# First norm's means on TensorE from a transposed X, and one new issue order up to the first convolution

## The chip, the cores and the metric

The kernel runs on one core of one Trainium2 chip. The time is the device time of that core in microseconds (us) for one launch: of the kernel before, three runs took 423.18, 423.9 and 425.21 us, with a median of 423.9.

## What is computed

Two pairs of layers on a sequence x of S = 2048 tokens with D = 512 channels (one batch). Each layer adds to x its function of the layer norm of x, with no learned scale:

```python
x = x + A(layernorm(x)); x = x + B(layernorm(x))      # twice, same weights

def A(u):      # state space layer: a long convolution per channel
    dt = exp(log_dt)[:, None]
    K = einsum("dn,dnl,dn->dl", C, exp((dt * A)[:, :, None] * l), dt * B).real   # D x 2048, 128 complex states
    return irfft(rfft(pad(u)) * rfft(pad(K)))[:2048] + u * Dskip

def B(x):      # attention: 32 heads of 16, 8 keys at distances 0, 2, .. 14 behind each token
    q, k, v = x @ wqkv
    return softmax(q . k[gathered] / 4, masked) . v[gathered] @ wo

def layernorm(x):
    m = mean(x); return (x - m) / sqrt(var(x) + 1e-5)
```

## The kernel before

**Layout.** x lies in four tiles X (128 x 4 x 512): token 16 p + j is row j of partition p, so that "row j" (j from 0 to 15) is a 128 x 512 slab. The normed rows go into tiles N of the same shape. The convolution of layer A is a two-stage Fourier transform: the first stage (L636) multiplies each row j by a table F1 on TensorE (PE); its result is copied into a large tile Z; then, by groups of channels, come transposes (L248), the second stage (L263), the product with the kernel's spectrum Kt (L275), and the way back (L291, L295 and the y rows at L336 to L344). The B layer begins with the copies at L1549.

**Generating the convolution kernel.** All that comes before the first convolution is in `kgen`. A ladder of squarings makes the powers of exp(dt A) up to 2048 (words m, q, l, b). From these, for each quarter c of 128 channels, tables U and V are built by doubling: DVE multiplies (L502, L504; for the last V steps, whose names end in n, L483), and the real and imaginary sums are either added on DVE (L514, words that begin with %), or summed by PE with an identity matrix (L528, words with +) and copied back by ACT (L535, L538, words with =). U and V have two buffers, so quarters 2 and 3 write where quarters 0 and 1 were read. The products lie in Z's space until the tables are done; so no z copy may come before the last table word.

Then PE multiplies V by U (words p{c}{q}, L568 and L572, four per quarter); ACT copies two products at a time out to KT (k{c}{m}, L579). The second k of a quarter also issues four transfers of KT to DRAM, two on SP and two on POOL (L587), and POOL, behind them, one transfer back into the tile `rows` (L590). The spectra s{c}{i} (L601, L606) multiply rows by tables G0 and G1 on PE; o and e copy and combine them (ACT L617, L622 to L625, DVE L630) and store them on SP (L611). Spectra 1 to 6 take ten matmuls (L601) and one ACT copy; the others five (L606), an ACT copy and two DVE sums.

**The first norm.** Statistics of row j are word n{j}: on DVE by bn_stats (L179 to L181), or, with an a behind it, on ACT in two passes, one that sums the row into its mean (L184), one that sums the squares of the differences (L185). r0 and r1 make the inverse deviation of eight rows each (ACT, L190 and L191), a0 and a1 the bias (DVE, L196); N{j} applies both to a row (ACT L202 or DVE L204). f{j} is the first stage on PE, z{j} its copy to Z (DVE L641, ACT L643 for halves, ACT L645 whole).

**The order of the work.** It is written by hand in the string KGEN (L353 to L370). `run` (L769) takes its words one by one within a manual schedule and issues the instructions of each; so the order of the string is the order on each engine, and an instruction that waits holds all behind it on the same engine. Words that begin with @ are the steps of the first convolution: @T0 is the first transpose. Words w and W are matmuls on the identity that write a PSUM tile ahead of its use (L550 to L556).

**Loads.** After the parameters, SP's queue issues X (L144), F1 (L1663) and G1 (L419); G0 follows at the word prep (L447). The weights and constants of later layers come on SP and POOL.

Of the kernel before, what the change touches and what calls it, by code (L numbers as in the profile page):

```python
# [14 lines left out]
F32 = mybir.dt.float32  # L15
# [160 lines left out]
def first_norm_row(nc, small, st, Xg, j, on_act):  # L176
    x, mv = Xg[j // 4][:, j % 4, :], st["mv"][:, j, :]
    if not on_act:
        nc.vector.bn_stats(st["stats"][:, j, :], x)  # L179
# [4 lines left out]
    nc.scalar.activation(junk[:], x, ACT.Identity, scale=1.0 / D, accum_out=mv[:, 0:1])  # L184
    nc.scalar.activation(junk[:], x, ACT.Square, scale=-1.0, bias=mv[:, 0:1], accum_out=st["m2"][:, j:j + 1])  # L185
# [130 lines left out]
def a_layer(nc, tc, C, Xg, Ng, kt_dram, layer, Z, es_z, a=None):  # L316
# [10 lines left out]
    def y_rows(g, hf, row, ps, add):  # L327
# [25 lines left out]
KGEN = ("m0 q0 b0 x1 l0 m1 q1 x0 t l1 b1 x3 x2 q2 m2 b2 l2 x5 m3 U4p:1 q3 U4:0 l3 b3 %U4:0 u:1 m4 q4 u:0 l4 b4 m5 q5 U2p:0 l5 +U2p:0 b5 "  # L353
# [30 lines left out]
def kgen(nc, tc, C, prm, kt_dram, Zf, norm_row, norm_rstd, norm_apply, norm_apply_row, norm_tiles, load_rest, es_a, es_y, open_conv):  # L384
    everything = KGEN.split()
    with ExitStack() as es:
# [32 lines left out]
        nc.sync.dma_start(Gt[1][:], C["G_h"].ap()[1])  # L419
# [89 lines left out]

        def sum_dve(name, c):  # L510
            prod, out, hn, f, size = sums[name, c]
            for r in range(2):
                x, y = (prod[i][:, (r + i) % 2].rearrange("n (h f c) -> n h f c", h=hn, f=f) for i in range(2))
                nc.vector.tensor_tensor(out(r), x, y, ALU.add if r else ALU.subtract)  # L514
# [35 lines left out]
        def warm(tile, cols):  # L550

            flat = tile[:].rearrange("n a b -> n (a b)")
            while cols > 0:
                n = min(cols, 512)
                nc.tensor.matmul(flat[:, 0:n], C["ident"][:], C["ident"][:].unsqueeze(1).to_broadcast([128, n // 128, 128]), start=True, stop=True)
                cols -= n  # L556
# [18 lines left out]
        def product_out(c, m):  # L575
# [3 lines left out]
            nc.scalar.copy(KT[:, :, :, m * 16:(m + 1) * 16, :].rearrange("v w t h f -> v (w t) h f"),  # L579
# [5 lines left out]
            for t in range(2):  # L585
                for b in range(2):
# [4 lines left out]
                                                   C["rows_dram"].ap()[c].rearrange("t b w v x -> (w v) (t b) x"))  # L591

# [40 lines left out]
        def first_stage(j):  # L633
            ps = tiles["f", j] = psum()[0].tile([128, 2, D], F32, name="ps_s1", tag="psk")
            for r in range(2):
                nc.tensor.matmul(ps[:, r, :], C["F1"][:, j, r, :], C["Ng"][j // 4][:, j % 4, :], start=True, stop=True)  # L636

        def first_stage_out(j, part):
            src = tiles["f", j][:].rearrange("k r (c e g) -> k r c g e", c=16, e=GE)
            if part == "v":  # L640
                nc.vector.tensor_copy(C["z_view"][:, 1, j], src[:, 1])  # L641
            elif part == "a":
                nc.scalar.copy(C["z_view"][:, 0, j], src[:, 0])  # L643
            else:
                nc.scalar.copy(C["z_view"][:, :, j], src)  # L645

# [40 lines left out]
        for c in range(4):  # L687
# [48 lines left out]
        for j in range(16):  # L736
            for a in ("", "a"):
                word(f"N{j}{a}", lambda j=j, a=a: norm_apply_row(j, bool(a)), f"a{j // 8}", "prep")
            word(f"n{j}", lambda j=j: norm_row(j, False))
            word(f"n{j}a", lambda j=j: norm_row(j, True))  # L740
        tables = [w for c in range(4) for w in in_quarter(c, *steps)]
        for j in range(16):
            word(f"f{j}", lambda j=j: first_stage(j), f"N{j}a" if f"N{j}a" in everything else f"N{j}")
            for part in ("", "a", "v"):
                word(f"z{j}{part}", lambda j=j, part=part: first_stage_out(j, part), f"f{j}", *tables)
        for full in everything:
            if full[0] in "wW":
                word(full, lambda full=full: warm((product_tile if full[0] == "w" else spectrum_tile)(int(full[1]), int(full[2])), int(full.split(":")[1])), "x5")
# [866 lines left out]
def kernel(  # L1615
# [40 lines left out]
    n1 = {}  # L1656

    def load_rest():
# [4 lines left out]
        nc.sync.dma_start(C["F1"][:], C["F1_h"].ap())  # L1663
# [65 lines left out]
```

## Time and profile before

| what | us |
|---|---|
| median of three runs | 423.9 |
| the profiled execution | 424.25 |
| its span, first to last instruction | 422.4 |
| first ACT statistics row (L184) begins | 45.92 |
| first spectrum (L601) begins | 69.55 |
| first transpose of the convolution (L248) begins | 119.53 |
| first copy of the B layer (L1549) begins | 153.69 |

The mean granted clock of TensorE in that execution was 0.992 of full speed. Engines are named PE (TensorE matmul), PEld (its weight load), DVE (VectorE), ACT (ScalarE), POOL (GpSimd) and SP (SyncE, which issues transfers); a q behind a name is its instruction queue. A row of the timeline has the start, the duration, the engine, the line, the operation, the tiles written and read with shapes, and a count; in square brackets the idle time before it and what ended that. A row of groups has the total busy time, the mean of one in ns, and the idle time before. In the windows view each row is a stretch of time with the busy time of each engine in it.

### The profile page before, as it was taken

The numbers are of one execution on the slowest core, as the hardware profiler recorded it, in microseconds if no ns is written. First come the engines' busy times: TensorE is split into PE (matmuls) and PEld (weight loads), VectorE is DVE, ScalarE is ACT, GpSimd is POOL, SyncE is SP. The second block draws the span as 40 slices with busy tenths as digits, with TensorE's granted clock in tenths as the row PEclk, the third lists the DMA queues.
The fourth block names the chain that finished last, engine by engine and source line by source line (L and its number), as shares of the span: only waits on it lengthen the run. The fifth ranks groups of instructions, "written<-read, shape, count | busy, mean of one in ns | idle before, by whom it ended". The sixth has DMA issues, their size and how long they took to land.

```text
span 422.4 us, 12235 instructions
## 1 busy us (share of the span) xinstructions
PE 379.3 (90%) x5120; PEld 259.1 (61%) x5120; DVE 398.4 (94%) x730; ACT 332.7 (79%) x600; POOL 26.0 (6%) x68
## 2 busy tenths in 40 slices
PE   1157898999989999999999999889999999997996
PEld 1023585676458755587866575278855686875663
DVE  5999999999889979899999999999989999999994
ACT  6999998998979989766665699989988676663542
POOL 5000011001210000002020000000000001200000
PEclk9999999999999999999999999999999999998999
DMA  8900001254889960005480028239300009350022
GB/s 241 424 29 0 2 12 42 76 166 104 250 245 276 259 213 2 2 2 98 81 174 3 2 64 238 102 107 288 107 0 4 2 2 166 73 115 2 2 102 101
DMA packets 25822, 44.09 MB, mean 104 GB/s; under 512 B 7317, under 2 KB 17238, under 8 KB 25126
## 3 DMA queue, kind: packets, MB, share of 16 engines
q1 hardware_dynamic: 22918, 38.09, 31.9%
q0 software_dynamic: 1888, 4.56, 5.0%
q8 instruction: 40, 0.66, 0.6%
q10 hardware_dynamic: 960, 0.66, 0.5%
q14 instruction: 16, 0.13, 0.1%
HBM read 29.04 MB, written 6.95 MB: 85 GB/s over the span
## 4 chain that ended last, share of the span: by engine, by line
PE 46%; DVE 25%; ACT 7%; DMA 6%; issue 4%; SPq 2%; DVEq 0%; ACTq 0%
PE ps_qk L1207 10%; DVE prodpv L1403 9%; PE ps_v L1294 5%; DVE prodqk L1257 4%; PE vp L291 3%; PE psg L601 3%; PE Lp L1279 3%; PE po L1413 3%; PE ps_o L1443 2%; DVE Z L504 2%; DVE pab L275 2%; DMA Kt<-kt_scratch 2%; PE psk L568 2%; DMA V<-V 2%; ACT Z L1496 2%
## 5 line engine op out<-in xcount | busy, mean ns | idle before, releaser
L1403 DVE TENSOR_TENSOR prodpv<-V,Lsb 128x2048 bf16<-128x2048 bf16 x64 | 75.3, 1221 | 0.7 <-DMA V<-V 0.4
L1207 PE MATMUL ps_qk<-xnT,wqk 128*128 128x512 bf16 x256 | 59.9, 379 | 0.0
L1255 DVE TENSOR_TENSOR prodqk<-qT,N 128x1024 bf16<-128x1024 bf16 (+3 forms) x88 | 42.6, 544 | 1.9 <-ACT N L1210 1.9
L1257 DVE TENSOR_TENSOR prodqk<-qT,N 128x1024 bf16<-128x1024 bf16 (+3 forms) x56 | 40.4, 765 | 0.3 <-ACT qT L1210 0.2
L1413 PEld LDWEIGHTS <-prodpv 128*128 128x128 bf16 x1024 | 35.3, 100 | 7.2 <-DVE prodpv L1403 2.0
L275 DVE TENSOR_TENSOR pab<-xc,Kt 128x2048 bf16<-128x2048 bf16 (+1 forms) x34 | 38.8, 1154 | 0.7 <-issue 0.4
L1413 PE MATMUL po<-halves,prodpv 128*128 128x64 bf16 x1024 | 38.1, 196 | 0.9 <-DVE prodpv L1403 0.9
L1207 PEld LDWEIGHTS <-wqk 128*128 128x128 bf16 x256 | 23.7, 98 | 23.5
L269 ACT CAST xc<-xp 128x1024 bf16<-128x1024 f32 (+1 forms) x34 | 34.6, 1033 | 2.2 <-PE xp L263 1.9
L291 PEld LDWEIGHTS <-pab 128*128 128x128 bf16 x512 | 30.4, 98 | 7.0 <-DVE pab L275 3.5
L291 PE MATMUL vp<-sb_IC,pab 128*128 128x128 bf16 x512 | 33.6, 219 | 0.6 <-DVE pab L275 0.3
L1279 PEld LDWEIGHTS <-prodqk 128*128 128x128 bf16 x1024 | 29.8, 96 | 5.5 <-DVE prodqk L1257 2.5
L295 ACT CAST VT<-vp 128x1024 bf16<-128x1024 f32 (+1 forms) x31 | 32.7, 1065 | 0.6 <-PE vp L291 0.6
L1443 PE MATMUL ps_o<-wo_t,oT 128*128 128x512 bf16 x128 | 33.0, 379 | 0.0
L1279 PE MATMUL Lp<-sb_bones,prodqk 128*128 128x8 bf16 x1024 | 30.5, 166 | 1.0 <-DVE prodqk L1257 0.8
L528 PE MATMUL psadd<-Z,sb_ident 128*128 128x384 bf16 (+3 forms) x75 | 18.7, 337 | 13.1 <-DVE Z L504 7.9
L1294 PE MATMUL ps_v<-wv,xnT 128*128 128x256 bf16 x256 | 30.4, 272 | 0.0
L1424 ACT CAST oT<-po 128x512 bf16<-128x512 f32 x32 | 17.7, 589 | 13.8 <-PE po L1413 13.7
L1210 ACT CAST N<-ps_qk 128x512 bf16<-128x512 f32 x32 | 18.7, 587 | 12.1 <-PE ps_qk L1207 11.9
L1160 DVE BATCH_NORM_STATS2 ln_stats<-X 128x6 f32<-128x512 bf16 x39 | 24.9, 682 | 2.7 <-ACT X L1549 2.7
L1301 ACT CAST V<-ps_v 128x512 bf16<-128x512 f32 x32 | 18.2, 588 | 10.9 <-PE ps_v L1294 10.8
L1294 PEld LDWEIGHTS <-xnT 128*128 128x128 bf16 x256 | 24.2, 98 | 3.2
(202 smaller groups left out, 837.8 us busy)
## 6 DMA issues: line engine op xcount, KB each, us to landing
Kt<-kt_scratch SPq DMA_DIRECT2D x60, 256.0 KB, 5.5
kt_scratch<-ks SPq DMA_DIRECT2D x32, 128.0 KB, 3.0
G<-c_G SPq DMA_DIRECT2D x2, 1536.0 KB
V<-V SPq DMA_DIRECT2D x8, 288.0 KB, 7.8
X<-in_A_u_dram SPq DMA_DIRECT2D x4, 512.0 KB, 4.8
F1Tsb<-c_F1T SPq DMA_DIRECT2D x2, 1024.0 KB
V<-V SPq DMA_DIRECT2D x4, 512.0 KB
V<-V POOLq DMA_DIRECT2D x4, 384.0 KB, 8.3
```

Source lines behind the costliest of these rows:

```text
L269: nc.scalar.copy(xcs[cg][:, gs].rearrange("q g o l -> q (g o l)"), xps[cg][:].rearrange("q h n -> q (h n)")[:, gs.start * 128:gs.stop * 128])
L275: nc.vector.tensor_tensor(pabs[cg][:, gs], xcs[cg][:, gs].to_broadcast([128, gs.stop - gs.start, 2, 128]), kts[cg][:, gs], ALU.mult)
L291: a.last_pe = nc.tensor.matmul(vp[:, g, :], pabs[cg][:, gs.start + g, ab, :], C["IC"][:, ab, :], start=(ab == 0), stop=(ab == 1))
L295: copy(dst[..., parts(cg)[part]], vps.pop((cg, part))[:].rearrange("k g (q e) -> k q e g", e=GE))
L1207: nc.tensor.matmul(t.ps[:], wqk[:, ct, f0:f0 + 128], x_group(g)[:, :, ct], start=(ct == 0), stop=(ct == 3))
L1255: nc.vector.tensor_tensor(b.pr[:, u:u + 2 * n, 1 - halves_of[0], :], q, cols(kT[i][:, starts[0]:starts[0] + n * 128]), ALU.mult)
L1257: nc.vector.tensor_tensor(b.pr[:, u:u + 2 * n].rearrange("f u a q -> f a u q")[:, ::-1], q.unsqueeze(1).to_broadcast([128, 2, 2 * n, 64]), ...
L1279: nc.tensor.matmul(t.Lp[:, w, u % 2, u // 2, :], b.pr[:, u].rearrange("f a q -> f (a q)"), bones[:], start=False, stop=(t.parts == W // 2 ...
L1294: nc.tensor.matmul(t.ps[:, jj, :], tokens(ct, jp * 2 + jj, c), wv[:, ct, fp * 256:(fp + 1) * 256], start=(jj + ct == 0), stop=(jj == 1 and ...
L1403: nc.vector.tensor_tensor(t.p2[:, c:c + k, 0:nj, :].rearrange("p c j (d h) -> p c j d h", d=DH), m.V2[i // 2][:, c0 + c:c0 + c + k, r0:r0 ...
L1413: nc.tensor.matmul(po[jj // k][:, jj % k, c, :], t.p2[:, c - c0, jj, :], fold, start=(first and c == c0 and jj % k == 0), stop=(last and c ...
L1443: nc.tensor.matmul(t["ps"][:], m.oT[:, ft, j * 128:(j + 1) * 128], wo_t[:, ft, :], start=(start and ft == lo), stop=(ft == 3 or kept and f ...
```

## The change

1. The ACT pass that made the mean of a row (L184) is gone. Instead, sixteen transposing transfers on SP, issued behind the loads of X, write each row j transposed (512 channels by 128 tokens, in four blocks) into space that G1 (rows 0 to 11) and F1 (rows 12 to 15) take later. A new word xm sums them: 64 matmuls, each with a 128 x 128 block as weights and one column of ones, four of them added up per row, into one PSUM tile of 16 columns. A new word xo copies that to the means with a scale of 1/512 on ACT, and then issues the loads of G1 and F1 on SP. The norm rows, the spectra and the first stage wait for xo. All 16 norm rows are on ACT now (15 and one on DVE before).
2. The identity matmuls that fill PE are given as `~columns` and are issued with the next fresh PSUM tile: 8,704 columns, where there were 14,720.
3. Thirteen N rows are on ACT and three on DVE (8 and 8 before); of the z copies by halves, ten are on ACT and six on DVE (8 and 8), with each half to be placed by itself. One table copy (u:1) goes from DVE to ACT, one (B:0) from ACT to DVE. k may be given to DVE by a letter, which the new order doesn't do.
4. The string KGEN is new from its first word to the end of the first convolution.

The places of the order of which the prediction speaks, before:

```
... v16xn:0 p02 n14a +0U512p:1 +1U512p:1 v16x:1 n0a n2 =1U512p:1 l10 prep p00 n4a
k01 v16yn:1 =0U512p:1 p01 %v16x:1 v2:2 n1a U4p:2 Aa:2 %v2:2 p12 k00 c0 +U4p:2 ua:2 =U4p:2 v4p:2 Ba:2 U2:2 %U2:2 p13 +v4p:2 n6a
U256:2 k11 p10 =v4p:2 U1p:2 p11 w23:256 %U256:2 v2p:3 n7a +v2p:3 r0 =v2p:3 +U1p:2 Aa:3 v8p:2 =U1p:2 U1024:2 k10 U4:3 s01 ua:3
%U1024:2 +1v8p:2 o01 v4:3 %U4:3 a0 ...
... v16xn:2 N3a +U1024p:3 %U1:3 =U1024p:3 N5a p22 v8:3 o10 k21 U512:3 p21 n13a %v8:3 N1a %U512:3 p20 n11a k20 v16x:3 s11 n10a %v16x:3
s13 o11 o13 p31 r1 v16y:3 N6a a1 p30 N0a %v16y:3 k30 s00 N12 N13 f6 N8 N11 z6 p32 o00 e13 p33 N15a f1 k31 ... z2v s31 o30 @T0
```

and after:

```
... %U512:0 xm xo n2a v16yn:0 prep +1v8p:1 +0v8p:1 U512p:1 n5a =1v8p:1 n3a =0v8p:1 n9a v16x:1 v16xn:0 p02 p03 p00
+0U512p:1 n14a k01 n0a +1U512p:1 =0U512p:1 =1U512p:1 p01 v2:2 U4p:2 %v2:2 v16yn:1 n4a p13 +U4p:2 ua:2 n1a Aa:2 =U4p:2 v4p:2 U2:2
%v16x:1 %U2:2 n6a k00 n7a s01 o01 r0 c0 n8a p12 +v4p:2 p10 =v4p:2 Ba:2 n12a k11 s03 o03 U256:2 a0 ...
... a1 %v8:3 N14a %U512:3 v16yn:2 N12a v16x:3 v16y:3 %v16x:3 %v16y:3 v16xn:2 p22 p20 p21 p23 k20 N6a s11 k21
N13a o11 N8a N3a N15a s13 p33 p32 p31 p30 k31 f12 s00 o13 k30 ... f0 z0 z141a @T0
```

The diff, cut to its core:

```diff
     junk = small.tile([128, D], BF, name="n1_junk", tag="junk", bufs=1)
-    nc.scalar.activation(junk[:], x, ACT.Identity, scale=1.0 / D, accum_out=mv[:, 0:1])
     nc.scalar.activation(junk[:], x, ACT.Square, scale=-1.0, bias=mv[:, 0:1], accum_out=st["m2"][:, j:j + 1])
...
         load_rest()
-        nc.sync.dma_start(Gt[1][:], C["G_h"].ap()[1])
+        flat = [Gt[1][:].rearrange("n a b -> n (a b)"), C["F1"][:].rearrange("n a b c -> n (a b c)")]
+        xT = [flat[j // 12][:, j % 12 * D:(j % 12 + 1) * D].rearrange("n (t p) -> n t p", t=4) for j in range(NJ)]
+        for j in range(NJ):
+            nc.sync.dma_start_transpose(xT[j], C["x_row"](j))
...
+        def fresh(tile):
+            warm(tile, late.pop("fill", 0))
+            return tile
...
+        def row_sums():
+
+            ps = tiles["m"] = fresh(psum()[1].tile([128, 2, 512], F32, name="psm", tag="psg"))
+            for j in range(NJ):
+                for t in range(4):
+                    nc.tensor.matmul(ps[:, 0, j:j + 1], xT[j][:, t, :], C["signs"][:, 0:1], start=(j + t == 0), stop=(j == NJ - 1 and t == 3))
+
+        def row_sums_out():
+            nc.scalar.activation(C["mean"](), tiles["m"][:, 0, 0:NJ], ACT.Copy, scale=1.0 / D)
+            nc.sync.dma_start(Gt[1][:], C["G_h"].ap()[1])
+            nc.sync.dma_start(C["F1"][:], C["F1_h"].ap())
+        word("xm", row_sums, "x5")
+        word("xo", row_sums_out, "xm")
...
-            word(f"n{j}", lambda j=j: norm_row(j, False))
-            word(f"n{j}a", lambda j=j: norm_row(j, True))
+            word(f"n{j}", lambda j=j: norm_row(j, False), "xo")
+            word(f"n{j}a", lambda j=j: norm_row(j, True), "xo")
...
-        nc.sync.dma_start(C["F1"][:], C["F1_h"].ap())
```

More of the change, by code (lines that the diff above doesn't have):

```diff
@@ L508, in step, with warm @@
                 C["powers_used"] = last
+        def warm(tile, cols):
+            flat = tile[:].rearrange("n a b -> n (a b)")
+            while cols > 0:
+                n = min(cols, 512)
+                nc.tensor.matmul(flat[:, 0:n], C["ident"][:], C["ident"][:].unsqueeze(1).to_broadcast([128, n // 128, 128]), start=True, stop=True)
+                cols -= n
+        def fresh(tile):
+            warm(tile, late.pop("fill", 0))
+            return tile
         def sum_dve(name, c):
@@ L546, in spectrum_tile @@
             if ("s", c, i) not in tiles:
-                tiles["s", c, i] = psum()[1].tile([128, 2, 512], F32, name="psg", tag="psg")
+                tiles["s", c, i] = fresh(psum()[1].tile([128, 2, 512], F32, name="psg", tag="psg"))
             return tiles["s", c, i]
[L550 to L556, printed above, removed]
         def product(c, q):
@@ L573, in product, with product_out @@
                                          skip[:, s0 + hl - 7:s0 + hl + 1, :], start=False, stop=False)
-        def product_out(c, m):
+        def product_out(c, m, copy):
             if ("KT", c) not in tiles:
@@ L633, in first_stage @@
         def first_stage(j):
-            ps = tiles["f", j] = psum()[0].tile([128, 2, D], F32, name="ps_s1", tag="psk")
+            ps = tiles["f", j] = fresh(psum()[0].tile([128, 2, D], F32, name="ps_s1", tag="psk"))
             for r in range(2):
@@ L639, in first_stage_out @@
             src = tiles["f", j][:].rearrange("k r (c e g) -> k r c g e", c=16, e=GE)
[L640 to L644, printed above, removed]
+            if not part:
                 nc.scalar.copy(C["z_view"][:, :, j], src)
+                return
+            r = int(part[0])
+            (nc.scalar.copy if part[1] == "a" else nc.vector.tensor_copy)(C["z_view"][:, r, j], src[:, r])
         word("y", lambda: nc.scalar.copy(Ln[:], lads[7][:, 1, :]), "l6")
@@ L725, in kgen @@
             for m in range(2):
-                word(f"k{c}{m}", lambda c=c, m=m: product_out(c, m), f"p{c}{2 * m}", f"p{c}{2 * m + 1}", "prep")
+                for v, copy in (("", nc.scalar.copy), ("v", nc.vector.tensor_copy)):
+                    word(f"k{c}{m}{v}", lambda c=c, m=m, copy=copy: product_out(c, m, copy), f"p{c}{2 * m}", f"p{c}{2 * m + 1}", "prep")
             for i in range(4):
-                word(f"s{c}{i}", lambda c=c, i=i: spectrum(c, i), f"k{c}0", f"k{c}1")
+                word(f"s{c}{i}", lambda c=c, i=i: spectrum(c, i), *[w for w in everything if w.rstrip("v") in (f"k{c}0", f"k{c}1")], "xo")
                 word(f"o{c}{i}", lambda c=c, i=i: spectrum_odd(c, i), f"s{c}{i}")
@@ L1656 @@
     n1 = {}
+    C["x_row"] = lambda j: Xg[j // 4][:, j % 4, :]
+    C["mean"] = lambda: n1["st"]["mv"][:, :, 0]
     def load_rest():
```

16 lines of the change are left out of this document (8 added, 8 removed), and 33 rows, old and new, of the table KGEN.

## The prediction

> **What bounds the kernel now.** First the busy totals of the page, for the whole span; then the windows view, because a total is a mean over stages; then single rows of the timeline where the change puts a wait.
>
> ```profile
> PE 379.3 (90%) x5120; PEld 259.1 (61%) x5120; DVE 398.4 (94%) x730; ACT 332.7 (79%) x600; POOL 26.0 (6%) x68
> ```
>
> ```profile
> core 0: us, PE busy (x) PEld busy (x) DVE busy (x) ACT busy (x) POOL busy (x), PEclk, DMA share, GB/s
> 50.00:60.00 10.00, 10.00 (x289) 9.00 (x289) 9.93 (x17) 9.77 (x23) 0.00 (x0) 1.00 0.01 3
> 90.00:100.00 10.00, 10.00 (x183) 7.22 (x180) 9.97 (x18) 9.04 (x22) 1.87 (x3) 1.00 0.64 189
> 110.00:120.00 10.00, 9.39 (x48) 4.39 (x46) 8.39 (x14) 8.58 (x15) 0.57 (x3) 1.00 0.89 264
> ```
>
> The change touches only what lies ahead of the first convolution's end. There, from 50 to 100 us, DVE is never free (9.93 and 9.97 of 10 us), ACT nearly so, and PE is full. A stage in which three engines are all full has no slack for a wait that stops all three; removing work from one of them gives only what the other two can follow. Five rows mark the stage: the last DVE table product, the first spectrum behind it, the first transpose of the convolution (@T0), its first ACT copy, and the first ACT copy of the B layer.
>
> ```profile
> 97.65 1.23 DVE L514 TENSOR_TENSOR Vtab<-Z 128x960 bf16<-128x960 bf16 x2
> 98.22 1.27 PE L606 MATMUL psg<-G,rows 128*128 128x512 bf16 x5
> 119.53 1.07 PE L248 MATMUL pt<-sb_ident,Z 128*128 128x128 bf16 x16 [0.23 <-DVE Z L641]
> 121.69 1.01 ACT L269 CAST xc<-xp 128x1024 bf16<-128x1024 f32 x1 [1.22 <-PE xp L263]
> 153.69 1.01 ACT L1549 CAST X<-ps_y 128x1024 bf16<-128x1024 f32 x1 [0.72 <-PE ps_y L344]
> ```
>
> So the tables end at 97.65 + 1.23 = 98.9 us, @T0 follows 20.6 us later, and the B layer 34.2 us after that. The profiled execution took 424.25 us (span 422.4 and 1.85 around it), 0.35 over the median of 423.9; the sum starts from 424.25.
>
> **The change part by part.**
>
> *Work removed and added.* Groups of instructions of the first 153 us:
>
> ```profile
> L184 ACT ACTIVATE n_junk<-X 128x512 bf16<-128x512 bf16 x15 | 9.5, 636 | 0.1
> L184 ACT ACTIVATION_READ_ACCUMULATOR n_junk<-X 128x1 f32 x15 | 3.0, 198 | 0.0
> L185 ACT ACTIVATE n_junk<-X,n_mv 128x512 bf16<-128x512 bf16 x15 | 10.8, 723 | 0.5
> L202 ACT ACTIVATE N<-X,n_nb,n_rstd 128x512 bf16<-128x512 bf16 x8 | 6.3, 809 | 0.0
> L204 DVE TENSOR_SCALAR N<-X,n_rstd,n_nb 128x512 bf16<-128x512 bf16 x8 | 2.9, 418 | 0.0
> L641 DVE CAST Z<-ps_s 128x512 bf16<-128x512 f32 x8 | 5.4, 690 | 2.8 <-ACT Z L643 2.6
> L643 ACT CAST Z<-ps_s 128x512 bf16<-128x512 f32 x8 | 4.7, 595 | 1.2 <-PE ps_s L636 0.8 <-DVE Z L641 0.4
> L645 ACT CAST Z<-ps_s 128x1024 bf16<-128x1024 f32 x8 | 8.1, 1032 | 0.8 <-PE ps_s L636 0.8
> L625 ACT COPY odd<-psg 128x512 f32<-128x512 f32 x9 | 5.3, 594 | 0.9 <-PE psg L606 0.8
> L579 ACT CAST KT<-psk 128x640 bf16<-128x640 f32 x8 | 5.5, 682 | 0.0
> L671 PE MATMUL psc<-cl,signs 128*1 128x128 bf16 x8 | 0.6, 222 | 0.0
> L179 DVE BATCH_NORM_STATS2 n_stats<-X 128x6 f32<-128x512 bf16 x1 | 0.7, 718 | 0.0
> L483 DVE TENSOR_TENSOR Vtab<-Vtab,Z 128x960 bf16<-128x960 bf16 x10 | 6.7, 668 | 0.0
> ```
>
> ACT loses both L184 rows, 9.5 + 3.0 = 12.5 us; it gains five N rows (5 x 0.81 = 4.0), one more row at L185 (0.7), two half z copies (2 x 0.6 = 1.2) and the copy of the means, on 16 columns, some 0.3 as the 8-column L190 row below. That is about -6. DVE loses the bn_stats row (0.7), five N rows (5 x 0.42 = 2.1) and two z halves (2 x 0.69 = 1.4), and takes one table copy from ACT while it gives one away: about -4, of which only some 0.7 lies ahead of its last table product, because the N and z copies moved away stand behind it. PE gains 64 one-column matmuls; the nearest row, L671, has one column of weights and 128 moving columns and took 0.22 us, so they cost between nothing and 14 us; I take some 2, as a single column is moved, and they replace part of the roughly 6,000 warm-up columns that go. If ACT or DVE alone set the end, the stage would end 4 to 6 us earlier.
>
> *The transposes.*
>
> ```profile
> 4.22 2.21 SPq L144 DMA_DIRECT2D X<-in_A_u_dram  x4
> 45.92 0.69 ACT L184 ACTIVATE n_junk<-X 128x512 bf16<-128x512 bf16 x1
> ```
>
> ```profile
> X<-in_A_u_dram SPq DMA_DIRECT2D x4, 512.0 KB, 4.8
> V<-V SPq DMA_DIRECT2D x8, 288.0 KB, 7.8
> ```
>
> X is issued by 6.4 us and lands 4.8 later, at 11.2. The first statistics row stood at 45.9, and the new order asks for the means there, so sixteen 128 KB transposes have 35 us, 2.2 each. No row shows a transpose. Below: sixteen hidden copies like X's, 2 MB in 4.8 us from the last issue, cost nothing. Above: the nearest SBUF-to-SBUF row takes 7.8 us; sixteen one after the other would take 125, end at 136 and hold the path some 89 us. [...] I take nothing. The Trainium skill, "Advanced Engine Details and Errata", section "X-Bar Transpose (TRN2)", puts transposing DMAs at 350-400 GB/s; by it 2 MB would take an estimated 6 us, and late transposes, a rival below, would have no chance at all. No row of before shows a transpose, so the rival keeps the chance that it has from the 7.8 us row. The loads of G1 and F1, which wait for the means on SP, and of G0, queued behind them there, are 4 MB after some 47 us; DMA moved 3 GB/s from 50 to 60 us in the window above, so they land well ahead of the first spectrum. No cost.
>
> *The first spectrum, s01, moved up to the word behind k00.* The product's copy to KT starts a trip through DRAM (L587 out, L590 back) that s01 waits for.
>
> ```profile
> 60.47 0.68 PE L568 MATMUL psk<-Utab,Vtab 128*64 128x40 bf16 x16
> 60.77 0.67 ACT L579 CAST KT<-psk 128x640 bf16<-128x640 f32 x1
> 61.57 0.41 DVE L514 TENSOR_TENSOR Vtab<-Z 128x128 bf16<-128x128 bf16 x2
> 66.61 0.77 POOL L590 DMA_DIRECT2D rows<-rows_scratch  x1 [3.74 <-DMA rows_scratch<-KT]
> 67.58 0.30 ACT L190 ACTIVATE n_den<-n_m,eps 128x8 f32<-128x8 f32 x1
> 67.91 0.21 ACT L191 ACTIVATE n_rstd<-n_den 128x8 f32<-128x8 f32 x1
> 69.55 2.35 PE L601 MATMUL psg<-G,rows 128*128 128x512 bf16 x10
> 71.94 1.01 ACT L617 CAST ks<-psg 128x1024 bf16<-128x1024 f32 x1 [0.34 <-PE psg L601]
> ```
>
> Before, KT was done at 60.77 + 0.67 = 61.44 and s01 began at 69.55: a trip of 8.1 us, during which PE did eight words (p13, p10, p11 and sums among them), ACT and DVE theirs. In the new order PE has nothing between +U4p:2 and s01; p12, +v4p:2, p10 stand behind it. ACT has one n row, then o01, the copy of s01; behind o01 stands r0, the rstd; and a0 on DVE waits for r0. So from KT's end to a0 pass 8.1 + 2.4 (s01) + 1.0 (o01) + 0.5 (r0) = 12.0 us, and DVE owns about 2.6 in them (the lag product of L663 and U256:2). DVE stalls 9.4 us, and ACT and PE with it, so no engine catches up.
>
> The Trainium skill, "DMA: Bandwidth & Descriptors", section "Anatomy of one DMA — SWDGE (gpsimd) path", puts a DMA at a fixed 2 us plus its bytes; by it the two hops would be an estimated 4 to 5 us and this term 3 to 4 smaller. The trip measured here disagrees, with the return alone held 3.7 us by the way out, so the sum stays with 8.1.
>
> *The waits ahead of it.* %v2:2 overwrites the V table that p00 and p01 read. Before, v16x:1, v16yn:1 and %v16x:1 stood on DVE between v16xn:0, which frees p00, and %v2:2, and it started at 61.57, just behind p01's last matmuls (60.47 + 0.68). Now only v2:2 and U4p:2 stand there, 1.0 us, and p00, two sums and p01 take 2 + 0.9 + 2 = 4.9 (the pitch of a product is in the rows below): DVE waits 3.9. Next, U2:2 waits for =U4p:2, a copy on ACT behind a PE sum that stands behind p13, which waits for v16yn:1: about 0.9. With the 9.4, DVE reaches a0 14.2 us late. After it, smaller waits of the same kind (%U4:3 behind p11, v4:3 behind ACT's copy, U512:3 and a1) come to 1 + 1.5 + 1.5; I take 3.8. Less DVE's own 0.7, the tables end at 98.9 + 17.3 = 116.2 us.
>
> *The tail behind the tables.*
>
> ```profile
> 87.29 1.67 PE psk L568 x56
> 89.27 1.67 PE psk L568 x56
> 91.25 1.51 PE psk L568 x48
> ```
>
> ```profile
> 99.96 1.01 ACT L645 CAST Z<-ps_s 128x1024 bf16<-128x1024 f32 x1 [0.79 <-PE ps_s L636]
> 100.87 0.59 ACT L625 COPY odd<-psg 128x512 f32<-128x512 f32 x1
> ```
>
> The first rows, pieces of the chain of waits, show three products 1.98 us apart: quarter 2's were running at 87 to 93, well ahead of the tables' end. In the new order the last table word is v16xn:2 (4 x 0.67), which p20 and p21 need; p23, s11, s13 and all of p30 to p33 are queued behind them on PE. ACT's copy k20 can begin at tables' end + 0.9 (the rest of p20) + 2.0 = 2.9. From k20 to the last z ACT has in its order 4 KT copies (4 x 0.68), 6 N rows (6 x 0.81), one whole spectrum copy and a half (1.6), 10 odd copies (10 x 0.6), 10 half z (10 x 0.6) and 8 whole z (8 x 1.03): 29.3 us by busy time. The two timeline rows show that an ACT instruction begins about 0.1 before the one ahead ends (100.87 against 99.96 + 1.01), so 39 of them take some 3.6 less: 25.7. 2.9 + 25.7 = 28.6 without any wait. Before, ACT idled some 3 of the 20.6 us at the same place (the idle columns of L643, L645 and L625 above), and a third of that is added: 29.6. @T0 starts at 116.2 + 29.6 = 145.8, 26.3 later than 119.53. PE owes about 19 there and is not the bound.
>
> *The convolution.* ACT has 32.0 us of it from its first copy (121.69) to 153.69, with one L269 or L295 copy after the other in both orders. The new order asks for some y rows earlier: I take -1.
>
> Sum: 424.25 + 17.3 + 9.0 - 1.0 = 449.55, from 98.9 to 116.2, from 20.6 to 29.6, and the last. Rounded, **449.5 us**.
>
> **The rivals.**
>
> *Only one of the two waits shows.* If the trip of KT is covered (the engines reach k00 out of step, PE later than I think), only the tail is left: 424.25 + 9.0 - 1.0 - 0.7 = 431.6. If the tail is absorbed, because ACT's N rows and spectra find their data ready, only the 17.3 are left: 440.6. Against both: each engine runs its words in order, and o01 or k20 blocks whatever is ready behind it.
>
> *The transposes are late.* Two at a time would be 8 x 7.8 = 62 us, to 73.6: the means come 27 us late, ACT stops at the first n row and the s01 wait falls partly inside that. 449.5 + 27 - 9 = 467; serial, 424 + 89 = 513. [...] Against it: the 4.8 us of X's four.
>
> *It goes faster: DVE's relief is what counts.* If s01 and p20 cost nothing, all that is left is that ACT has 6 us and DVE 4 us less to do in a stage in which both were full; the later engine decides, so 424.25 - 4 = 420.5. This decides where KT's trip is at most the 2.6 us that DVE owns there, or the order is by time rather than by row. Against it stands the 8.1 measured.
>
> *The change does not do what it says.* The Identity passes do go from ACT, and DMAs do replace them; so only the amount can be small. Then time within 0.5%.
>
> **How the numbers follow.** Both waits show, 438 to 458: 0.63. One of them only, 430 to 441: 0.18. Transposes late, 458 to 515: 0.10. Relief wins, 418 to 422: 0.06. Nothing to be told apart: 0.03. A measurement of this kernel can tell about 0.5%, 2.1 us, from no change. The range leaves out the late transposes but for their start, and the relief: 431 to 461. The chances are 0.06 faster, 0.03 within 0.5%, 0.91 slower.
>
> **What would show it.** In the changed kernel: the L601 matmuls of the first spectrum idle some 8 us for rows, with ACT's L617 copy and DVE's n_nb row behind them; DVE's L514 idle 4 us at %v2:2; DVE's last table product (L483) at about 116; 29 to 30 us from there to the first L248; the means' copy near 47 us with no idle time for the transposes. Wrong if the trip is under 3 us, if PE finds other work ahead of s01, if ACT is idle less than I count because it had fallen behind, or if the means come late.

## The result and the profile after

The changed kernel took **479.7 us** (median of four runs, 478.68 to 480.09) against 424.1 before: ratio 1.131, 95% interval 1.127 to 1.134. The forecast had 449.5 and 431 to 461: slower was right, by far too little. The time splits by four instants of the two traces (end of the last DVE table product, first transpose of the convolution, first copy of the B layer, end):

| stage, us | before | after | change measured | change forecast |
|---|---|---|---|---|
| start to the tables' end | 98.9 | 117.9 | +19.0 | +17.3 |
| tables' end to @T0 | 20.7 | 37.5 | +16.9 | +9.0 |
| first convolution, @T0 to the B layer | 34.2 | 52.4 | +18.2 | -1.0 |
| all that follows | 268.7 | 270.4 | +1.7 | 0 |

Of the 30.5 us that the forecast lacked, 19.2 lie in the convolution, 7.9 in the tail behind the tables. The page's busy totals and then the windows view of the changed kernel (columns as before: PE, PEld, DVE, ACT, POOL, PEclk, DMA share, GB/s):

```profile
PE 393.3 (82%) x5128; PEld 269.6 (56%) x5170; DVE 396.3 (83%) x720; ACT 328.8 (69%) x580; POOL 26.1 (5%) x68
```

```profile
50.00:60.00 10.00, 9.66 (x171) 8.14 (x169) 6.77 (x12) 3.92 (x9) 0.00 (x0) 0.53 0.72 301
70.00:80.00 10.00, 3.82 (x9) 1.34 (x10) 2.21 (x5) 0.05 (x1) 1.53 (x3) 0.50 0.14 33
110.00:120.00 10.00, 4.56 (x95) 4.32 (x94) 7.92 (x12) 0.00 (x0) 0.00 (x0) 0.50 0.01 2
155.40:207.80 52.40, 34.33 (x422) 27.43 (x430) 32.06 (x38) 31.39 (x34) 0.00 (x0) 0.93 0.59 174
```

DVE and ACT did nearly as much work as before (396 for 398 us and 329 for 333); it is spread over 56 us more. From 70 to 80 us all three engines stand most of the time (busy for 3.8, 2.2 and 0.05 of 10 us). In the last row, the convolution, none of them is busy for more than 34.3 of 52.4 us: no engine bounds it, waits do. In the kernel before, PE, DVE and ACT were busy there for 32.0, 32.3 and 31.2 of 34.2 us. And the granted clock of TensorE is 0.50 to 0.53 in three of the rows; before, it was 1.00 from 40 to 160 us.

The timeline of the changed kernel, at the places that the prediction names:

```profile
25.81 5.19 SPq L420 DMA_TRANSPOSE F1sb<-X  x4
46.01 0.19 ACT L606 ACTIVATE n_mv<-psm 128x16 f32<-128x16 f32 x1 [0.37 <-PE psm L603]
61.25 0.27 DVE L527 TENSOR_TENSOR Vtab<-Z 128x128 bf16<-128x128 bf16 x1 [4.49 <-PE psk L573]
62.79 0.28 DVE L527 TENSOR_TENSOR Vtab<-Z 128x128 bf16<-128x128 bf16 x1 [1.27 <-PE psk L573]
68.10 0.76 DVE L505 TENSOR_TENSOR Z<-Utab,Z 128x512 bf16<-128x512 bf16 x2 [1.81 <-ACT Utab L551]
75.96 0.62 PE L620 MATMUL psg<-G,rows 128*128 128x512 bf16 x1 [8.38 <-DMA rows<-rows_scratch]
81.94 0.17 DVE L195 SCALAR_TENSOR_TENSOR n_nb<-n_mv,n_rstd 128x8 f32<-128x8 f32 x1 [9.74 <-ACT n_rstd L190]
122.61 0.69 ACT L584 CAST KT<-psk 128x640 bf16<-128x640 f32 x1 [15.37 <-PE psk L573]
155.44 1.07 PE L247 MATMUL pt<-sb_ident,Z 128*128 128x128 bf16 x16 [1.77 <-ACT Z L663]
207.83 1.01 ACT L1568 CAST X<-ps_y 128x1024 bf16<-128x1024 f32 x1 [0.72 <-PE ps_y L343]
```

The means came at 46.0, where the first statistics row had stood before; the transposes cost the path nothing. From there to the tables' end DVE stood for 20.1 us (0.2 before): 5.8 for p01 at %v2:2 (4.49 + 1.27), 1.8 at U2:2, 9.7 at a0, and 2.8 in smaller waits. Less some 1 us of work that DVE no longer has, that is the 19.0.

### The profile page after: what moved, and what is told of

Same layout as the page of the kernel before. It is cut to its first block, busy times and chain, and to the rows that moved or that the text cites. A ratio compares the mean times of both kernels' runs of the same rounds, so it can differ in the third digit from the quotient of the medians.

```text
span 478.2 us, 12281 instructions
## 1 busy us (share of the span) xinstructions
PE 393.3 (82%) x5128; PEld 269.6 (56%) x5170; DVE 396.3 (83%) x720; ACT 328.8 (69%) x580; POOL 26.1 (5%) x68
## 3 DMA queue, kind: packets, MB, share of 16 engines
q1 hardware_dynamic: 31622, 40.19, 30.5%
## 4 chain that ended last, share of the span: by engine, by line
PE 45%; DVE 14%; ACT 8%; issue 4%; DMA 3%; SPq 1%; DVEq 0%; ACTq 0%
PE ps_qk L1226 9%; PE vp L290 5%; DVE prodpv L1422 5%; PE ps_v L1313 4%; PE po L1432 4%; PE Lp L1298 4%; PE ps_o L1462 3%; DVE prodqk L1276 3%; DVE pab L274 3%; PE psk L573 2%; PE pt L247 2%; ACT xc L268 2%; DMA V<-V 2%; ACT Z L1515 2%; PE ps_y L343 2%
## 5 line engine op out<-in xcount | busy, mean ns | idle before, releaser
L290 PE MATMUL vp<-sb_IC,pab 128*128 128x128 bf16 x512 | 35.5, 225 | 17.9 <-DVE pab L274 17.2
L290 PEld LDWEIGHTS <-pab 128*128 128x128 bf16 x512 | 31.6, 101 | 25.6 <-DVE pab L274 22.1
L294 ACT CAST VT<-vp 128x1024 bf16<-128x1024 f32 (+1 forms) x31 | 31.4, 1024 | 17.1 <-PE vp L290 17.0
L1432 PEld LDWEIGHTS <-prodpv 128*128 128x128 bf16 x1024 | 34.6, 99 | 7.8 <-DVE prodpv L1422 2.2
L1432 PE MATMUL po<-halves,prodpv 128*128 128x64 bf16 x1024 | 37.5, 194 | 1.2 <-DVE prodpv L1422 1.1
L268 ACT CAST xc<-xp 128x1024 bf16<-128x1024 f32 (+1 forms) x34 | 33.4, 994 | 3.7 <-PE xp L262 3.4
L573 PE MATMUL psk<-Utab,Vtab 128*64 128x40 bf16 x512 | 25.3, 204 | 12.8 <-DVE Vtab L484 12.7
L573 PEld LDWEIGHTS <-Vtab 128*64 128x64 bf16 x512 | 23.2, 133 | 16.6 <-DVE Vtab L484 11.6
L253 DVE COPY zt<-pt 128x1024 bf16<-128x1024 bf16 x29 | 19.8, 686 | 14.7 <-PE pt L247 14.6
L649 DVE TENSOR_TENSOR ks<-psg,odd 128x512 bf16<-128x512 f32 x19 | 12.2, 682 | 19.1 <-ACT odd L644 19.0
L541 PE MATMUL psadd<-Z,sb_ident 128*128 128x512 bf16 (+3 forms) x74 | 20.1, 363 | 8.6 <-ACT Vtab L551 3.8
```

The lines of the kernel that those rows point to most:

```text
L268: nc.scalar.copy(xcs[cg][:, gs].rearrange("q g o l -> q (g o l)"), xps[cg][:].rearrange("q h n -> q (h n)")[:, gs.start * 128:gs.stop * 128])
L290: a.last_pe = nc.tensor.matmul(vp[:, g, :], pabs[cg][:, gs.start + g, ab, :], C["IC"][:, ab, :], start=(ab == 0), stop=(ab == 1))
L573: nc.tensor.matmul(ps[lanes, hl, 0:2 * NU], T[:, q * 16 + hl, r].rearrange("n v t -> n (v t)"), U[c % 2][:, q * 16 + hl, r, 0:NU].rearrang ...
L1432: nc.tensor.matmul(po[jj // k][:, jj % k, c, :], t.p2[:, c - c0, jj, :], fold, start=(first and c == c0 and jj % k == 0), stop=(last and c ...
```

## The experiments

All times in one table: each kernel's median, the end of its tables, the stretch from there to @T0 (tail), and the convolution, from the trace of one of its runs. Of e1, e2, e3, e4, e6, e10, e12, e13 and e16 there are only two runs each; those of e1, e2 and e4 lie 4.3 to 4.8 us apart, the others at most 3.1.

| run | us | tables' end | tail | convolution |
|---|---|---|---|---|
| before | 424.1 | 98.9 | 20.7 | 34.2 |
| after | 479.7 | 117.9 | 37.5 | 52.4 |
| e1 after, old convolution order | 463.1 | 118.2 | 37.6 | 33.5 |
| e2 before, new convolution order | 444.1 | 98.6 | 20.5 | 52.2 |
| e3 after, s01 later | 476.4 | 116.1 | 37.6 | 52.4 |
| e4 after, fill in the waits | 474.9 | 116.9 | 33.4 | 52.5 |
| e5 before, means only | 424.0 | 99.1 | 20.5 | 33.7 |
| e6 after, tail words earlier | 471.6 | 118.1 | 28.4 | 50.8 |
| e7 e5, rows early | 427.2 | 101.2 | 21.3 | 34.7 |
| e8 before, s01 early | 435.0 | 109.8 | 19.8 | 33.8 |
| e9 before, no fill | 424.3 | 100.3 | 20.5 | 33.4 |
| e10 after, four edits | 458.0 | 123.4 | 28.3 | 34.3 |
| e11 e5, one sum on PE | 427.7 | 102.4 | 20.5 | 33.9 |
| e12 e2, v a step later | 435.3 | 98.9 | 20.5 | 46.8 |
| e13 before, v behind own p | 455.5 | 98.9 | 20.5 | 64.6 |
| e14 before, p behind own c | 426.7 | 98.6 | 20.5 | 37.0 |
| e15 e5, sum earlier | 424.5 | 98.4 | 21.0 | 33.6 |
| e16 e2, p and v later | 430.3 | 98.3 | 20.5 | 39.8 |
| e17 before, %v2:2 behind p01 | 427.8 | 101.0 | 20.8 | 34.6 |

### The convolution's order, both ways (e1, e2)

```diff
 e1: after
-@T0 @t0 @T1 @t1 @X0 @c0 @T2 @T3 @k4 e31 ... @I15      (new order)
+@T0 @k4 @T1 @t0 e31 @t1 @X0 @c0 @T2 @t2 ... @I15      (order of before)
 e2: before, with the opposite edit
```

> The changed kernel with the convolution steps (from @T0 on) in the order of the kernel before. After took 52.4 us from its first L247 to its first L1568 copy, before 34.2. Theory: the new convolution order itself makes PE, DVE and ACT wait for one another in turn; then this kernel takes 34 to 37 us there and about 479.7 - 17 = 463 in all. Rival: what comes ahead (late spectra, late Kt loads, the lower clock) makes the convolution slow whatever its order; then it stays near 50 us there and 478 in all.

> The kernel before with only the convolution steps of the new order. Theory (the order itself is slow): 424 + 15 to 18 = 439 to 442, with some 50 us from the first L248 to the first L1549. Rival (the stage ahead makes it slow): 424 to 427.

e1: 463.1 us, 33.5 in the convolution. e2: 444.1 us (ratio to before 1.049, 1.035 to 1.062), 52.2 there. The new order alone brings the 18 us, whatever stands ahead of it; in e2 the granted clock was 0.97 in the convolution, so the clock does not make it either.

### Which neighbours in the order (e12, e13, e14, e16)

The timeline of the changed kernel shows how one step of the convolution goes:

```profile
168.57 1.22 DVE L274 TENSOR_TENSOR pab<-xc,Kt 128x2048 bf16<-128x2048 bf16 x1 [0.78 <-ACT xc L268]
169.85 1.75 PE L290 MATMUL vp<-sb_IC,pab 128*128 128x128 bf16 x16 [2.58 <-DVE pab L274]
171.39 1.06 PE L247 MATMUL pt<-sb_ident,Z 128*128 128x128 bf16 x8
171.63 1.01 ACT L294 CAST VT<-vp 128x1024 bf16<-128x1024 f32 x1 [3.10 <-PE vp L290]
172.24 1.06 PE L262 MATMUL xp<-zt,sb_C 128*128 128x512 bf16 x2
172.49 0.69 DVE L253 COPY zt<-pt 128x1024 bf16<-128x1024 bf16 x1 [2.69 <-PE pt L247]
```

PE stands 2.6 us at v for DVE's product p; the next transpose T is queued behind v; DVE stands 2.7 us for T at its copy t; and the next p is queued behind t. Each engine waits for what the other has queued behind its own wait. In the order of before one or two groups lie between p and v. The view of waits (total, times, longest) has these two waits in the convolution, first before, then after:

```profile
PE vp L291 <- DVE pab L275: 0.3, 1, 0.3
DVE zt L254 <- PE pt L248: 0.8, 1, 0.8
```

```profile
PE vp L290 <- DVE pab L274: 17.2, 11, 3.1
DVE zt L253 <- PE pt L247: 13.4, 10, 2.7
```

The two overlap in time and are not to be added. PE's wait alone is nearly as long as the 18.2 us that the convolution lost.

```diff
 e12: e2, for the groups g = 0 to 12
-... @c4 @k8 @v2 @T7 @t6 @p4 @Y1 @t7 @V2 @X5 @c5 @v4 @V4 @T8 ...
+... @c4 @k8 @T7 @t6 @p4 @v3 @V3 @Y1 @t7 @X5 @c5 @T8 ...
 e13: before
-... @X3 @v1 @c3 @T6 @V1 @X4 @v2 @t6 @p3 @k8 @c4 ...
+... @X3 @c3 @T6 @X4 @t6 @p3 @v3 @V3 @k8 @c4 ...
 e14: before
-... @c3 @T6 @V1 @X4 @v2 @t6 @p3 @k8 @c4 @T7 ...
+... @c3 @p3 @T6 @V1 @X4 @v2 @t6 @k8 @c4 @p4 @T7 ...
 e16: e2
-... @X3 @c3 @k7 @p3 @v3 @V3 @T6 @X4 @c4 @k8 @v2 @T7 ...
+... @X3 @v1 @p2 @c3 @V1 @k7 @T6 @X4 @v2 @p3 @c4 @V2 @k8 @T7 ...
```

> The kernel before with the new convolution order (444.1 us), in which only the way-back matmuls v and copies V of the first thirteen groups are taken out and put behind the product p of the next group; the transposes, y rows and all else stay. Theory: in the new order v of a group stands directly behind its own p, with the next transpose T behind v on PE and its copy t ahead of the next p on DVE, a loop p, v, T, t in which DVE and PE wait for each other (1.2 + 1.1 + 0.6 + 0.7 = 3.6 us a step against the measured 52.2 / 16 = 3.3); with v a step later the loop is cut, and the convolution falls from 52 to 35 to 39 us, 427 to 431 in all. Rival: the y rows or the late k loads of the new order make it slow; then 440 to 444.

> The kernel before; in its convolution only v and V of groups 0 to 12 are moved to directly behind the product p of the same group (before, one or two groups later). Theory (PE then holds the next transposes behind v, which waits for DVE's p, and DVE waits for those transposes): the convolution goes from 34.2 to 44 to 52 us, 434 to 442 in all. Rival (the distance of v from p is not what counts, since only 5 us came back in the new order): 424 to 429.

> The kernel before; in its convolution only the products p of groups 1 to 12 are moved to directly behind ACT's copy c of the same group (before, one or two words of DVE's work stood between). Theory (DVE then waits for c, 1.0 us and PE's X ahead of it, with the copies t behind): the convolution goes from 34.2 to 38 to 46 us, 428 to 436. Rival: DVE has work enough, 423 to 426.

> The kernel before with the new convolution order in which both are spread: p of a group stands behind the X of the next group, v behind the X of the one after, V behind the next c; transposes T, copies t, y rows and loads stay as in the new order. Theory (the short distances of v and p are all of the 18 us): 34 to 38 us in the convolution, 424 to 428 in all. Rival (transposes, y rows or loads of the new order cost by themselves): 430 to 438.

e13 is the plainest: v directly behind its own p makes 64.6 us of before's 34.2 and 455.5 in all (ratio 1.074, 1.070 to 1.077), more than expected, with the same two waits, which the view of waits of e13 (119 to 172 us) shows:

```profile
PE vp L291 <- DVE pab L275: 17.0, 12, 3.3
DVE zt L254 <- PE pt L248: 13.5, 8, 2.8
```

A part of e13's loss is the clock: it was 0.89 in that stretch (1.00 before), and PE was busy there for 38.8 us instead of 32.0.

e14 costs 2.8 us in the convolution (426.7), less than expected: DVE mostly had other work. In the new order, v a step later gives back 5.4 us (e12, short of the 13 to 17 expected) and p and v together 12.4 (e16: 39.8, short of the 14 to 18 expected). So a longer way from c to p and from p to v gives back some two thirds of the loss. The remaining 5.6 us of e16 were not taken apart: transposes, copies, y rows and loads still stand as in the new order, PE still waits 5.2 us for p, and which of them costs it is not shown.

### The first spectrum (e3, e8)

```diff
 e3: after
-k00 n7a s01 o01 r0 c0 n8a p12 +v4p:2 p10 =v4p:2 Ba:2 n12a k11 s03 o03 U256:2 a0 ... p11 k10
+k00 n7a r0 c0 n8a p12 +v4p:2 p10 =v4p:2 Ba:2 n12a k11 s01 o01 U256:2 a0 ... p11 k10 s03 o03
 e8: before
-p12 k00 c0 +U4p:2 ... k10 U4:3 s01 ua:3 %U1024:2 +1v8p:2 o01
+p12 k00 s01 o01 c0 +U4p:2 ... k10 U4:3 ua:3 %U1024:2 +1v8p:2
```

> The changed kernel with s01 and o01 moved behind k11, and s03 and o03 behind k10; p12, +v4p:2, p10 and their copies now stand ahead of s01 on PE and ACT. Theory: s01 behind k00 holds PE for the trip of KT (9.2 us idle before s01 in after, DVE 9.7 us before n_nb); moved, a0 comes 7 to 9 us earlier, TensorE's clock drops less, and the time falls by 7 to 11 us to 469 to 473. Rival: the wait is only a cover for later ones (the c=2 tables, p2x) and the gain is given back: 477 to 480.

> The kernel before with only s01 and o01 moved to directly behind k00; nothing else. Theory (the trip of KT through DRAM, 8.1 us, is paid where nothing stands between on the same engines): PE and ACT stand some 6 us at s01 and o01 and DVE soon after, 424 + 5 to 8 = 429 to 432. Rival (the other engines' queues absorb it): 423 to 426.

e8: 435.0 us (ratio 1.027, 1.020 to 1.034), above the 429 to 432 expected. The move of one spectrum costs the kernel before 10.9 us at the tables' end. In its timeline s01 waits 7 us, then runs for 4.46 us instead of the 2.35 of before, since the clock had fallen to 0.50 while PE stood (64 to 72 us), and DVE loses 10.8:

```profile
68.19 4.46 PE L601 MATMUL psg<-G,rows 128*128 128x512 bf16 x10 [6.96 <-DMA rows<-rows_scratch]
74.40 0.76 DVE L504 TENSOR_TENSOR Z<-Utab,Z 128x512 bf16<-128x512 bf16 x2 [10.82 <-ACT Utab L538]
```

In the changed kernel itself, e3 brought a0 from 81.9 to 73.3 as expected, but the tables' end only from 117.9 to 116.1, and the time to 476.4. That is near the rival's 477 to 480: the next waits took the place of the one removed, at a clock of 0.50 from 70 to 80 us and 0.85 from 80 to 90, as the timeline of e3 shows:

```profile
82.46 0.50 DVE L498 TENSOR_TENSOR Z<-cb,Z 128x256 bf16<-128x256 bf16 x2 [3.87 <-PE psadd L542]
89.36 1.11 DVE L506 TENSOR_TENSOR Z<-Vtab,Z 128x768 bf16<-128x768 bf16 x2 [3.90 <-ACT Vtab L552]
```

### The wait for p01 (e17)

```diff
 before
-v16xn:0 p02 n14a +0U512p:1 +1U512p:1 v16x:1 n0a n2 ... k01 v16yn:1 =0U512p:1 p01 %v16x:1 v2:2 n1a U4p:2 Aa:2 %v2:2 p12
+v16x:1 v16xn:0 p02 n14a +0U512p:1 +1U512p:1 n0a n2 ... k01 =0U512p:1 p01 v2:2 n1a U4p:2 Aa:2 %v2:2 v16yn:1 %v16x:1 p12
```

> The kernel before with only v16x:1 moved ahead of v16xn:0, and v16yn:1 and %v16x:1 moved behind %v2:2, as in the new order: 3.9 us of DVE work no longer stand between v16xn:0 and %v2:2. Theory: DVE waits there for p00, two sums and p01 at full clock, 3.9 us, and the tables end 3.5 to 4.5 us later: 427 to 429. If the wait is 5.8 as in after, the order alone makes it, 429 to 431. Rival: DVE's wait is absorbed behind it: 423 to 425.

427.8 us (ratio 1.009, 1.006 to 1.012), tables' end 2.1 later, but the wait at %v2:2 was only 0.66 us: the run kept DVE's statistics row and a ladder step between v16xn:0 and v2:2 (1.7 us), and both sums ahead of p00, so it imitates the new order badly. It shows that this order costs something, and says nothing of the 3.9.

The run of e6 (below) says more, though it was made for another question: its order is that of after far beyond this place, but its clock was 0.98 from 50 to 60 us, where after had 0.53. The two sums took 1.4 us in it (2.7 in after; 0.9 had been counted), and DVE waited 3.8 us at %v2:2, where 3.9 had been forecast:

```profile
58.84 0.27 DVE L528 TENSOR_TENSOR Vtab<-Z 128x128 bf16<-128x128 bf16 x1 [2.52 <-PE psk L574]
60.38 0.28 DVE L528 TENSOR_TENSOR Vtab<-Z 128x128 bf16<-128x128 bf16 x1 [1.27 <-PE psk L574]
```

In after, e1, e3, e4 and e10, which have the same order there, the clock was 0.50 to 0.75 from 56 to 62 us (1.00 in e6), and the wait 5.8 to 6.0. So the order makes 3.8 us of this wait and the low clock 2.0. What kept the clock up in e6 is not shown.

### The tail (e6) and the clock (e4, e9)

```diff
 e6: after
-%U512:2 U1024p:3 %U1:3 +U1024p:3 N0a n10a =U1024p:3 ... v16yn:2 N12a v16x:3 ... v16xn:2 p22 p20 p21 p23 k20 N6a s11 k21
+%U512:2 v16yn:2 p22 p23 c2 k21 U1024p:3 %U1:3 +U1024p:3 N0a n10a v16xn:2 p20 =U1024p:3 p21 k20 ... N12a v16x:3 ... N6a s11
 e4: after
+~6144 p02    ~16384 s01    ~12288 p22    ~12288 p20
 e9: before
-w03:1536 w03:128 w03:896 w03:384 w03:2688 w03:128 w03:384 w03:1536 w03:128 w03:512 w03:6144 w23:256
```

> The changed kernel with quarter 2's last table words and products earlier: v16yn:2, p22, p23, c2 and k21 behind %U512:2; v16xn:2, p20, p21 and k20 around =U1024p:3. After had its tables done at 117.9 us and its first L247 37.5 us later (before: 98.9 and 20.7). Theory: the tail is long because all of quarters 2 and 3 on PE stood behind the last table word; now 10 to 14 us of it go, 466 to 470 in all, and PE stands less, so that its clock holds. Rival: the tail is ACT's own 26 us of work, which this does not change, and the time falls by less than 4 us.

> The changed kernel with identity matmuls added where PE stood still: 6,144 columns ahead of p02, 16,384 ahead of s01, 12,288 ahead of each of p22 and p20. No other order changes. Theory: part of the loss is TensorE's granted clock, which fell to 0.50 in the stretches 50 to 60, 64 to 80 and 106 to 128 us, behind stretches with PE idle; kept at work it stays at 1.0, the products behind (3.1 us each instead of 2.0) and the spectra (4.4 instead of 2.35) are short again, and the time falls by 6 to 10 us to some 470 to 474. Rival: the clock matters little, since PE waits there anyway: within 2 us of 479.7, or later by the columns added.

> The kernel before without its 14,720 columns of identity matmuls; no other change. Theory: they keep TensorE's clock up while PE would stand; without them the clock falls in the stretch from 40 to 60 us, the products of quarter 0 take some 3 us instead of 2, and DVE waits for them: 427 to 434. Rival: PE has enough to do by itself; 423 to 425, or less, as PE has 6 us less to do.

e6: the tail fell by 9.1 us to 28.4, and the time by 8.1 to 471.6, a little less than expected. Its clock was 0.54 from 118 to 130 us, as in after, so this gain comes from the order. e4: 474.9, 4.8 less, also a little short. Behind 110 us it held the clock, as its windows view shows against the row of 110 to 120 us above,

```profile
110.00:120.00 10.00, 8.88 (x157) 5.95 (x155) 6.87 (x11) 0.00 (x0) 0.00 (x0) 1.00 0.01 2
```

and the tail came to 33.4: with the clock held, it is 4.1 us shorter. The gain of the whole, 4.8, is little more than the 4.3 between e4's two runs, so its size is rough. e9 missed: the kernel before without its fill took 424.3 (ratio 1.002, 0.998 to 1.005). The clock did fall in it,

```profile
50.00:60.00 10.00, 9.78 (x193) 8.12 (x194) 9.93 (x18) 7.25 (x19) 0.00 (x0) 0.59 0.01 3
```

but DVE was busy for 9.93 of these 10 us all the same; the tables ended 1.4 us later, and the time cannot be told from that of before. In these two runs a low clock cost time where PE was waited for (the tail of after), and none that could be measured where DVE was full.

### All four edits together (e10)

```diff
 after, with the edits of e1, e3 and e6
+~6144 p02    ~6144 p22    ~6144 p20
```

> The changed kernel with four edits at once: the convolution in the order of before, s01 and s03 later, quarter 2's last table words and products earlier, and 6,144 columns of fill ahead of each of p02, p22 and p20. Theory (the four costs add up as measured one by one: -17, -3, -8, -2 to -5): 446 to 451. If the parts hide one another (what one wait gives back the next takes): 452 to 460; if they feed on one another through the clock, under 444.

458.0: the costs do not add up; the four gains together would have made 446.9. The convolution (34.3) and the tail (28.3) are as in e1 and e6, but the tables end at 123.4, later than in any other run. In this stage one wait gives way to another, as in e3: DVE's longest wait is now one that after did not have, at a1,

```profile
114.65 0.17 DVE L195 SCALAR_TENSOR_TENSOR n_nb<-n_mv,n_rstd 128x8 f32<-128x8 f32 x1 [4.88 <-ACT n_rstd L190]
```

where the copies k21 and k20 now stand on ACT ahead of r1.

### The means alone (e5, e7, e11, e15)

```diff
 e5: before, with the transposes, xm, xo and no Identity passes
-... +0v8p:1 w03:512 n5a U512:0 m10 ... n0a n2 =1U512p:1 ...
+... +0v8p:1 w03:512 xm xo n5a U512:0 m10 ... n0a n2a =1U512p:1 ...
 e7: e5, six n rows, r1 and a1 earlier, eight N rows from DVE to ACT, six of them ahead of the tables' end
 e11: e5
-w03:6144 p03 ... v16x:1 ... %v16x:1
+p03 ... v16xp:1 ... +0v16xp:1 l10 prep p00 =0v16xp:1 +1v16xp:1 ... p01 =1v16xp:1
 e15: e5
-%v2:2 p12 k00 c0 +U4p:2 ua:2 =U4p:2
+%v2:2 +U4p:2 p12 =U4p:2 k00 c0 ua:2
```

> The kernel before with its own order and fills, and only the means changed: sixteen transposes, the sums on PE, the copy of the means and the late loads of G1 and F1, placed ahead of the first norm row; the Identity passes are gone, and the one row that DVE had is on ACT. Theory: the loss of after lies in the order, not in the means; then this takes 420 to 424 (ACT has 12 us less to do, but DVE, the fuller engine, only 1). Rival: the transposes or the late loads cost by themselves: 428 or more.

> The kernel of the means alone with ACT's freed time put to use: six norm rows earlier, r1 and a1 earlier, and the eight N rows that DVE had moved to ACT, six of them ahead of the tables' end. DVE loses 8 x 0.42 = 3.3 us behind the tables. Theory: DVE sets the time up to the tables' end and PE behind it, so ACT's relief can be turned into little: 421 to 424. Rival: DVE decides behind the tables too, 419 to 421.

> The kernel of the means alone, with one table sum (v16x of quarter 1, 1.23 us on DVE) summed by PE and copied by ACT (two copies of 0.95) in ACT's freed time, and the fill of 6,144 columns ahead of p03 left out to make room for it. Theory (DVE sets the time up to the tables' end, ACT has room now): 422 to 423.5. Rival: PE's eight matmuls there delay quarter 0's products and DVE waits: 424.5 to 428.

> The kernel of the means alone with the PE sum +U4p:2 moved ahead of p12 and its copy ahead of k00, since the only wait of DVE between 44 and 100 us in that kernel was 1.6 us for this copy. Theory (DVE had lost the whole of what the means gave it, 1.0 us of bn_stats, at that wait): the tables end 1 to 1.5 us earlier, 422.0 to 423.0. Rival: the next wait takes its place, 423.3 to 424.5.

e5 took 424.0 (ratio 0.999, 0.996 to 1.002): the half of the change that gave it its name costs nothing and brings nothing that could be measured. Its windows view and timeline show why:

```profile
50.00:60.00 10.00, 9.95 (x276) 8.70 (x276) 10.00 (x19) 7.88 (x18) 0.00 (x0) 1.00 0.89 376
90.00:100.00 10.00, 9.89 (x182) 7.22 (x181) 9.97 (x17) 7.12 (x15) 1.87 (x3) 1.00 0.62 181
```

```profile
63.71 0.76 DVE L506 TENSOR_TENSOR Z<-Utab,Z 128x512 bf16<-128x512 bf16 x2 [1.58 <-ACT Utab L552]
```

ACT is down from 9.8 and 9.0 to 7.9 and 7.1 of 10 us, but DVE is as full as before, and the one us of statistics that it lost comes back as a wait of 1.6. e15 removed that wait, and the tables ended 0.7 earlier, but the time did not move (424.5 against 424.2, ratio 1.001, 1.000 to 1.003). e7 and e11 tried to put ACT's room to use and were slower by 0.8% and 1.0%, against the 421 to 424 and 422 to 423.5 expected: with six rows earlier on ACT s01 came 2.8 us later than in e5, and with a sum on PE DVE stood 3.6 us at %v2:2. No kernel here beats the one before.

## Why the prediction was wrong

**What bounds the kernel: right.** Three full engines leave no room; DVE's waits between 46 and 118 us make up the loss of that stage.

**Work removed: right in kind.** ACT's relief is real and worth nothing by itself (e5).

**The transposes: right that they are hidden.** They were slow, though: the last group of issues ends at 25.81 + 5.19 = 31.0 us, sixteen in 21 us. No row of before told how many of them move together; in after they were issued 1.3 us apart and landed 2.5 us after their issue, so they were done by 33.5, some 10 us before the sums on PE read them (44.2). The estimate of 6 us for them from the Trainium skill, "Advanced Engine Details and Errata", section "X-Bar Transpose (TRN2)", does not hold in this trace.

**s01: the wait right, its size in part by luck.** 9.7 us were forecast as 9.4, but from other parts: KT's trip took 6.6 us (69.3 to 75.96) instead of 8.1, s01 4.4 instead of 2.4, and the two errors nearly cancel. e8 shows the wait by itself.

**The waits ahead of it: the mechanism stands in the trace,** with 5.8 + 1.8 us against 3.9 + 0.9; the surplus is mostly PE at half clock, a term that the forecast did not have at all (in e6, at 1.00, the two are 3.8 + 1.2). The smaller waits were 2.8 for 3.8. Tables' end: 117.9 for 116.2.

**The tail: the mechanism right, its size not.** ACT's work from k20 on was 26.3 us for the 25.7 counted; but k20 began 4.7 us behind the tables' end instead of 2.9, and ACT stood 6.5 us instead of 1. Of these 7.9 us too few e4 gives 4.1 to the clock, the term that the forecast lacked; the rest was not taken apart. e6 confirms that the place of quarter 2's words is what makes the tail long: moving them took 9.1 us off it.

**The convolution: the step that failed.** The prediction says that "ACT has 32.0 us of it from its first copy (121.69) to 153.69, with one L269 or L295 copy after the other in both orders", and takes -1. ACT's work was indeed the same, 31.4 us; but in the new order it took 52.4 us to do it. The step fails where it takes the 32.0 us of the old order for what ACT's work alone needs in any order. That holds only while nothing makes ACT wait (it waited 0.3 us for v before, 16.8 after), and the new order's chain from p to v to T to t to the next p was not followed, though the words stand there: `@p3 @v3 @V3 @T6`. That the order costs the 18 us is shown by e1 and e2; that the distances from c to p and from p to v make some two thirds of them, by e16, with e12 and e13 for v alone; the last third stays open.

## What to carry to other kernels

The same work in another order took 52.4 us instead of 34.2 here, since each engine waited for what the other had queued behind its own wait. So a new order is to be read for the distance between a word and the word that needs it, also where no work is added. The relief of ACT brought nothing that could be measured while DVE was full (e5), and the two tries to use ACT's room made the kernel slower (e7, e11). And a wait that stops TensorE can have a second price behind it, the clock: 2.0 us at %v2:2, 4.1 in the tail.

## What the runs showed of the hardware

The granted clock was 0.50 in stretches in which PE stood much of the time (busy for 3.8 and 4.6 of 10 us in the rows of after from 70 and from 110 us), and ten matmuls of s01 took 4.46 us in e8 for 2.35 before. That agrees with the Trainium skill, "TensorE: Matmul & The Clock Gate", section "Part 1: The HAM clock gate (the "warmup" mystery)": the throttled state is the default and activity releases it. From 50 to 60 us, where after had 0.53, PE was busy for 9.7 of 10 us, behind ten with 7.6; which stand lowered the clock there is not shown. With fill the clock was 1.00 instead of 0.50 from 110 to 120 us (e4), but in e9 the whole fill of the kernel before was worth nothing that could be measured. The same order does not always get the same clock: from 50 to 60 us it was 0.53 in after and 0.98 in e6. A transposing DMA of 128 x 512 from SBUF to SBUF took 1.3 us of SP's queue each (5.19 for four) and 2.5 us to land.
